# Routed mixture kernel: the first 256 columns of each upward block without a branch, two arms past them in place of seven widths

## The chip, the cores and the metric

The kernel runs on one core of one Trainium2 chip, and the metric is the time of one execution in device microseconds. Engines are named as the profile names them: PE (TensorE matmul), PEld (its weight loads), DVE (VectorE), ACT (ScalarE), POOL (GpSimd), SP (SyncE, which here only issues transfers).

## The reference

Three layers follow one another; all arithmetic is in f32. The change touches only the last one, a mixture of eight experts that sends each of 2304 tokens to one expert, with room for 576 tokens in each.

```python
kv  = einsum('bhsd,bhse->bhde', k, v)            # linear attention, then an RMS norm
x   = rmsnorm(einsum('bhsd,bhde->bhse', q, kv)) * g_norm
x   = relu(x @ w_in)**2 @ w_out                  # 2304 tokens, 512 -> 2048 -> 512
expert_idx = argmax(x @ w_gate, axis=1)          # 8 experts, capacity 576
# tokens are put into disp[e, slot] in their order, those past the capacity are dropped
h   = maximum(einsum('ecd,edf->ecf', disp, w1), 0)   # w1: 8 x 512 x 1024
y   = einsum('ecf,efd->ecd', h, w2)                  # w2: 8 x 1024 x 512
out[i] = gate_w[i] * y[expert_idx[i], slot[i]]
```

How many tokens an expert holds is known only while the kernel runs. With the inputs that are timed, the experts hold, in the order in which the kernel works on them (positions 0 to 7), 576, 167, 219, 576, 160, 391, 76 and 52 tokens.

## The kernel before, in words

A float32 product is done in three passes of float32r matmuls (high by high, high by low, low by high), so a block of 512 input features is 4 x 3 = 12 matmuls into one stretch of PSUM. Attention and the first mixture fill the first 486 us. After that comes the second mixture, one expert after another.

For each expert the kernel does an "up" stage and a "down" stage. The up stage has eight blocks f = 0 to 7 of 128 hidden features, two in each call of `up2` (i = 0 to 3). `up` multiplies the block of `w1` by the transposed tokens `x2` into `hb`, a PSUM tile of two banks of 512 columns (three such tiles take turns), and `put_g` writes the result to `g2`: ACT makes the relu's high part of 576 columns, DVE the low part. `put_last` has ACT copy the last half tile to `gl`. After each call, `next_pair` (not after the last) has ACT cast a freshly loaded 128x512 pair of weights and POOL subtract the cast from it; SP loads into four staging buffers ahead of that. The down stage multiplies `g2` by `w2`, tile of tokens by tile, each scaled on ACT and scattered by POOL.

An expert of at most 128 tokens takes the other arm of `up2`: `turned` computes the block with the tokens as the stationary operand, and the result is turned back by a transpose. Position 0 is special: most of its first 256 columns are done early, and `up_rest` does what is past them (320 columns here).

The work past the first mixture is in a section where every engine follows the order of the code (`tc.manual_schedule`). So the order of each engine's queue is the order of the calls in the loop over experts at its end, and SP's is that of `load_x` and `next_pair`. A `tc.If` compares a register with a number on each engine that has work in the block, and jumps. Both arms of it stand in the engine's instruction stream one after the other. `nothing` is a matmul of eight columns that stands in an arm without work.

The choice of width in the kernel before: `LEVELS` (line 526) has seven widths, `widths` (lines 815 to 823) searches them by halving, and each end of the search is an arm with its own 12 matmuls (24 for 576 columns). Where an arm is wider than a bank, its first 256 columns lie at column 256 of `hb`, otherwise at column 0. A register (`off`, loaded from `off_i`) tells ACT and DVE where to read.

Of the kernel before, what the change touches and what calls it, by code (L numbers as in the profile page):

```python
# [10 lines left out]
I32 = mybir.dt.int32  # L11
I64 = mybir.dt.int64
AF = mybir.ActivationFunctionType
ALU = mybir.AluOpType
# [5 lines left out]
P = 128  # L20
# [6 lines left out]
def attn_moe_kernel(ctx: ExitStack, tc: tile.TileContext, cap, kp, vp, qt, gn, wm, wg, wgt, w1, w2, ident, tri, out):  # L27
    nc = tc.nc
    B, NPAIR, _, NCH, _ = kp.shape
# [5 lines left out]
    E, NF2 = w1.shape[0], w1.shape[1] * 2  # L35
# [6 lines left out]
    NARROW, BANK, HALF = 256, 512, P // 2  # L42
# [4 lines left out]
    const = ctx.enter_context(tc.tile_pool(name="const", bufs=1))  # L47
# [8 lines left out]
    tri_sb = const.tile([P, 2, P], BF16, name="tri_sb")  # L56
    cnt = const.tile([P, E], F32, name="cnt")
    cnt_i = const.tile([P, E], I32, name="cnt_i")
    off_i = const.tile([P, E], I32, name="off_i")
    last_i = const.tile([P, E], I32, name="last_i")  # L60

    ek_i = const.tile([P, E], I32, name="ek_i")
# [460 lines left out]

    LAG, LEAD = 2, 4
    HOT = 9
    LEVELS = (NARROW, 304, 352, 400, 448, BANK, cap)
    units = []

    with tc.manual_schedule(engines={mybir.EngineType.SP}):
# [146 lines left out]
        for s in range(len(units)):  # L676
            j, f = units[s]
# [37 lines left out]
        v = nc.vector  # L715
# [3 lines left out]
        v.tensor_scalar(cnt, cnt, 1.0, -1.0, op0=ALU.max, op1=ALU.add)  # L719
        v.tensor_copy(last_i, cnt)  # L720
        v.tensor_scalar(last_i, last_i, 7, 7, op0=ALU.logical_shift_right, op1=ALU.logical_shift_left)
        v.tensor_scalar(off_i, cnt, float(BANK - 1), float(BANK - NARROW), op0=ALU.is_gt, op1=ALU.mult)
    ph1.close()


# [8 lines left out]
    hb = [psum[0].tile([P, 2 * BANK], F32, name=f"hb{i}") for i in range(3)]  # L734
# [23 lines left out]
    with tc.manual_schedule():  # L758
# [9 lines left out]
        ET = mybir.EngineType  # L768
# [7 lines left out]
        def nothing(ps, w):  # L776

            nc.tensor.matmul(ps[:w, :E], lhsT=tri_sb[:, 0, :w], rhs=tri_sb[:, 1, :E], start=True, stop=True)
# [20 lines left out]
        def w1_at(e, i, a, c):  # L799

            return we1[e, 2 * i + c // 2][:, a, c % 2 * 2 * P:(c % 2 + 1) * 2 * P]

        def part(e, f, h, o, w, x=x2):


            order = [(c, a, m) for c in range(KD) for a, m in PASSES]
            if f == 0:
                order = [(c, a, m) for a, m in ((0, 0), (1, 0), (0, 1)) for c in range(KD)]
            for k, (c, a, m) in enumerate(order):
                nc.tensor.matmul(  # L810
                    h, lhsT=w1_at(e, f // 2, a, c)[:, f % 2 * P:(f % 2 + 1) * P], rhs=x[:, m, c, o:o + w],
                    start=k == 0, stop=k == 3 * KD - 1,
                )

        def widths(e, levels, arm):

            mid = len(levels) // 2
            if not mid:
                return arm(levels[0])
            with tc.If(n[e] > levels[mid - 1]) as c:  # L820
                widths(e, levels[mid:], arm)
            with c.Else():
                widths(e, levels[:mid], arm)

        def up(e, f):

            h = hb[(e * NF2 + f) % 3]

            def arm(w):
                if w > BANK:  # L830
                    part(e, f, h[:, BANK - NARROW:BANK], 0, NARROW)
                    part(e, f, h[:, BANK:BANK + w - NARROW], NARROW, w - NARROW)
                else:
                    part(e, f, h[:, :w], 0, w)

            widths(e, LEVELS, arm)
            put_g(f, h[:, bass.ds(off[e], cap)], slice(0, cap))

        turned_sb = [ht_p.tile([P, 2 * P], F32, name=f"turned{i}") for i in range(2)]

# [10 lines left out]
        def up2(e, i):  # L851

            with tc.If(nall[e] > P) as many:  # L853
                up(e, 2 * i)
                up(e, 2 * i + 1)
            with many.Else():
                if i == 0:
                    nc.scalar.copy(turned_sb[0], turned(e, 0))
                if i + 1 < NF2 // 2:
                    s = turned(e, i + 1)  # L860
                hs = [hb[(e * NF2 + 2 * i + k) % 3][:, :P] for k in range(2)]
                for k, h in enumerate(hs):
                    nc.tensor.transpose(h, turned_sb[i % 2][:, k * P:(k + 1) * P], id_sb)
                if i + 1 < NF2 // 2:
                    nc.scalar.copy(turned_sb[(i + 1) % 2], s)
                for k, h in enumerate(hs):
                    put_g(2 * i + k, h, slice(0, P))
            for f in range(2 * i, 2 * i + 2):
                put_last(f, bass.ds(last[e], HALF))

        def put_g(f, src, cols):

            g = g2[f][:, :, cols]
            nc.scalar.activation(out=g[:, 0], in_=src, func=AF.Relu)  # L874
            nc.vector.scalar_tensor_tensor(  # L875
                out=g[:, 1], in0=src, scalar=0.0, in1=f32(g[:, 0]), op0=ALU.max, op1=ALU.subtract
            )
# [74 lines left out]
        for f in range(3):  # L952
# [5 lines left out]
            skip_runtime_bounds_check_because="an expert has no more than all tokens",  # L958
        )
        _, n = nc.values_load_multi_w_load_instructions(  # L960
            cnt_i[0:1, :], engines=[PE], min_val=0, max_val=cap,
            skip_runtime_bounds_check_because="the counts are clamped to the capacity on the chip",
        )
        _, nall = nc.values_load_multi_w_load_instructions(
            cnt_i[0:1, :], engines=[PE, ET.Activation, ET.DVE, ET.Pool], min_val=0, max_val=cap,
            skip_runtime_bounds_check_because="the counts are clamped to the capacity on the chip",
        )

        _, off = nc.values_load_multi_w_load_instructions(
            off_i[0:1, :], engines=[ET.Activation, ET.DVE], min_val=0, max_val=BANK - NARROW,  # L970
            skip_runtime_bounds_check_because="the offsets are one of two numbers",
        )

        _, last = nc.values_load_multi_w_load_instructions(
            last_i[0:1, :], engines=[ET.Activation], min_val=0, max_val=(cap - 1) // P * P,
            skip_runtime_bounds_check_because="the counts are clamped to the capacity on the chip",
# [11 lines left out]
        for e in range(E):  # L988
# [3 lines left out]
            if e == 0:  # L992
                with tc.If(early > NARROW - 1) as done:
                    for f in range(NF2):
                        up_rest(f)
                with done.Else():
                    tr_x(0, 0)
                    tr_x(0, 1)
                    for f in range(NF2):
                        up(0, f)  # L1000
                        put_last(f, bass.ds(last[0], HALF))
            else:
                for i in range(NF2 // 2):
                    up2(e, i)
                    if i < NF2 // 2 - 1:
                        next_pair((AP, AP))
# [69 lines left out]
```

## Time and profile before

| what | us |
|---|---|
| median of 3 runs (810.14 to 811.97) | 810.14 |
| the profiled execution's own time | 804.85 |
| its span, from the first to the last instruction | 803.1 |
| PE busy in the span | 729.3 |
| DVE, ACT, POOL busy | 371.1, 310.5, 291.5 |

The profiled execution is 5.3 us shorter than the median of the runs. All durations below come from it; a difference worked out in it is put on the median. The second mixture takes the last 317 us of the span. There each expert's up stage and down stage can be told apart by the matmuls: those of line 810 (up), 846 and 863 (the turned arm), and 907 (down).

### The profile page before, as it was taken

How to read it: one execution, taken by the hardware profiler on the slowest of the kernel's cores; microseconds unless marked ns; L12 is line 12 of the kernel's file. 1: busy time of each engine (PE TensorE's matmuls, PEld its weight loads, DVE VectorE, ACT ScalarE, POOL GpSimd, SP SyncE). 2: the span in 40 equal slices, each digit the busy share in tenths (PEclk: the TensorE clock that was granted, in tenths of full speed). 3: DMA queues.
4: the chain of work that ended last, by engine and by line, in shares of the span. 5: the costliest groups of instructions: out<-in, count | busy, mean ns of one | idle time of the engine just before them, and what ended most of it. 6: DMA issues, size and time to landing. Idle time of an engine off the chain costs nothing. (4 is left out here: it accounts for less than half of the span.)

```text
span 803.1 us, 12019 instructions
## 1 busy us (share of the span) xinstructions
PE 729.3 (91%) x3988; PEld 648.0 (81%) x3988; DVE 371.1 (46%) x829; ACT 310.5 (39%) x650; POOL 291.5 (36%) x288
## 2 busy tenths in 40 slices
PE   6788999999999999999999899997879997879663
PEld 6777999989999998899989788876768976777553
DVE  2999767279924943494469434202212202221101
ACT  2555454242223322322334533424635444544422
POOL 2575233030212002102104923253847373667440
PEclk9899999999999999999999999999969999999779
DMA  9937898020212012001004723353444454455400
GB/s 332 373 123 275 290 302 292 27 76 1 105 69 77 1 66 83 27 1 53 13 1 158 233 97 106 100 165 109 143 164 148 165 154 136 129 182 164 152 20 11
DMA packets 38044, 102.82 MB, mean 128 GB/s; under 512 B 4451, under 2 KB 4707, under 8 KB 37920
## 3 DMA queue, kind: packets, MB, share of 16 engines
q1 hardware_dynamic: 34912, 91.99, 35.0%
q0 software_dynamic: 3008, 9.10, 3.0%
q8 instruction: 87, 1.43, 0.8%
q14 instruction: 37, 0.30, 0.1%
HBM read 77.78 MB, written 23.91 MB: 127 GB/s over the span
## 5 line engine op out<-in xcount | busy, mean ns | idle before, releaser
L273 PE MATMUL pk<-xT,w 128*128 128x384 f32 x1152 | 223.1, 341 | 7.5 <-POOL w L183 4.6
L292 PE MATMUL pk<-w,g 128*128 128x512 f32 x864 | 218.3, 394 | 2.5 <-ACT g L284 2.5
L273 PEld LDWEIGHTS pk<-xT,w 128*128 128x128 f32 x1152 | 201.6, 188 | 17.3 <-POOL w L183 5.9
L194 POOL TENSOR_TENSOR w<-st,w 128x512 fp32r<-128x512 f32 x128 | 161.2, 1294 | 120.2 <-ACT w L190 120.2
L292 PEld LDWEIGHTS pk<-w,g 128*128 128x128 f32 x864 | 160.2, 188 | 31.7 <-ACT g L284 3.1
L810 PE MATMUL hb<-x,w 128*128 128x256 f32 (+2 forms) x672 | 105.5, 316 | 24.5 <-issue 11.3
L810 PEld LDWEIGHTS hb<-x,w 128*128 128x128 f32 x672 | 99.4, 203 | 29.9 <-issue 14.4
L875 DVE SCALAR_TENSOR_TENSOR g<-hb,g 128x576 fp32r<-128x576 f32 (+3 forms) x72 | 41.4, 586 | 147.6 <-ACT g L874 147.6
L281 ACT ACTIVATE rr<-pk 128x384 f32<-128x384 f32 x96 | 47.1, 491 | 154.2 <-PE pk L273 154.0
L283 DVE TENSOR_TENSOR pk<-pk,rr 128x384 f32<-128x384 f32 x96 | 54.0, 563 | 75.0 <-ACT rr L281 74.2
L102 POOL DMA_INDIRECT disp<-y,sli x18 | 19.0, 1058 | 173.5 <-DVE sli L409 52.9
L354 DVE SCALAR_TENSOR_TENSOR junk<-y,wgb 128x512 f32<-128x512 f32 x120 | 77.9, 684 | 0.6 <-ACT y L312 0.6
L190 ACT CAST w<-st 128x512 fp32r<-128x512 f32 x128 | 71.5, 620 | 11.6 <-DMA st<-in_w 11.2
L284 ACT CAST g<-pk 128x384 fp32r<-128x384 f32 x96 | 46.0, 479 | 72.2 <-DVE pk L283 71.8
L285 DVE TENSOR_TENSOR g<-pk,g 128x384 fp32r<-128x384 f32 x96 | 53.3, 556 | 36.3 <-ACT g L284 36.1
L183 POOL TENSOR_TENSOR w<-cf,w 128x512 fp32r<-128x512 f32 x32 | 46.8, 1481 | 61.4 <-ACT w L182 56.8
L907 PE MATMUL hb<-w,g 128*128 128x512 f32 x264 | 65.8, 407 | 3.2 <-DVEq L946 2.9
L907 PEld LDWEIGHTS hb<-w,g 128*128 128x128 f32 x264 | 50.2, 194 | 15.3 <-DVEq L946 3.2
L874 ACT ACTIVATE g<-hb 128x576 fp32r (+3 forms) x72 | 36.1, 515 | 66.3 <-PE hb L810 63.4
L102 POOL DMA_INDIRECT out<-o,meta x22 | 21.3, 968 | 56.5 <-DVEq L1019 22.6
L923 DVE SCALAR_TENSOR_TENSOR o<-bk,meta,o 64x512 f32<-64x512 f32 x3 | 2.3, 751 | 70.5 <-ACT o L922 50.6
L239 POOL TENSOR_SCALAR ms<-ss 128x8 f32<-128x8 f32 x18 | 4.6, 253 | 76.2 <-DVE ss L237 75.9
(134 smaller groups left out, 651.6 us busy)
## 6 DMA issues: line engine op xcount, KB each, us to landing
st<-in_w SPq DMA_DIRECT2D x64, 512.0 KB, 3.9
st<-in_wm SPq DMA_DIRECT2D x32, 512.0 KB, 6.9
disp<-zrow SPq DMA_DIRECT2D x9, 1028.0 KB, 11.2
xr<-disp SPq DMA_DIRECT2D x32, 257.0 KB, 4.8
k<-in_kp SPq DMA_DIRECT2D x16, 320.0 KB, 4.4
v<-in_vp SPq DMA_DIRECT2D x16, 320.0 KB, 4.1
q<-in_qt SPq DMA_DIRECT2D x18, 256.0 KB, 3.2
out<-zrow SPq DMA_DIRECT2D x9, 512.0 KB, 8.3
```

Source lines behind the costliest of these rows:

```text
L183: nc.gpsimd.tensor_tensor(w[:, 1, :], o, f32(w[:, 0, :]), op=ALU.subtract)
L190: nc.scalar.copy(w[:, 0, :], s[:, i, :])
L194: e.tensor_tensor(w[:, 1, :], s[:, i, :], f32(w[:, 0, :]), op=ALU.subtract)
L273: nc.tensor.matmul(h, lhsT=wi[f][:, a, c * P:(c + 1) * P], rhs=xT[j][:, m, c, :], start=n == 0, stop=n == 3 * KD - 1,)
L281: nc.scalar.activation(out=r, in_=h, func=AF.Relu)
L283: nc.vector.tensor_tensor(h, h, r, op=ALU.mult)
L284: nc.scalar.copy(g[:, 0, :], h)
L285: nc.vector.tensor_tensor(g[:, 1, :], h, f32(g[:, 0, :]), op=ALU.subtract)
L292: nc.tensor.matmul(ysets[j == 1][i], lhsT=g[:, a, i * P:(i + 1) * P], rhs=wo[f][:, m, :], start=f == 0 and n == 0, stop=f == NF - 1 and n ...
L354: nc.vector.scalar_tensor_tensor(out=junk, in0=yt[j * TB + i][:, :DM], scalar=1.0, in1=wgb[e // 2][:, e % 2, :], op0=ALU.mult, op1=ALU.mul ...
L810: nc.tensor.matmul(h, lhsT=w1_at(e, f // 2, a, c)[:, f % 2 * P:(f % 2 + 1) * P], rhs=x[:, m, c, o:o + w], start=k == 0, stop=k == 3 * KD - 1,)
L907: nc.tensor.matmul(ps[:k, :], lhsT=lhs(f, a), rhs=we2[e, f][:, b, :], start=n == 0, stop=n == len(passes) * NF2 - 1,)
```

## The change

Every up block of more than 128 tokens first does columns 0 to 255 without a branch. Then it asks whether the expert holds more than 256 tokens. If so, one of two arms does the next 160 (up to 416 tokens) or 320 columns; if not, a matmul of eight columns stands there. The first 256 columns always lie at column 256 of `hb`, so the register `off` and its loads go, and `put_g` reads at a fixed place. Widths in use for these inputs: 256 at positions 1, 2 and 4 as before; 256 and 320 at position 3 as before; at position 5 (391 tokens) 256 and 160 in place of 400.

```diff
-    off_i = const.tile([P, E], I32, name="off_i")
...
-    LEVELS = (NARROW, 304, 352, 400, 448, BANK, cap)
+    MIDDLE = 416
...
-        v.tensor_scalar(off_i, cnt, float(BANK - 1), float(BANK - NARROW), op0=ALU.is_gt, op1=ALU.mult)
...
-        def widths(e, levels, arm):
-
-            mid = len(levels) // 2
-            if not mid:
-                return arm(levels[0])
-            with tc.If(n[e] > levels[mid - 1]) as c:
-                widths(e, levels[mid:], arm)
-            with c.Else():
-                widths(e, levels[:mid], arm)
-
         def up(e, f):
 
-            h = hb[(e * NF2 + f) % 3]
-
-            def arm(w):
-                if w > BANK:
-                    part(e, f, h[:, BANK - NARROW:BANK], 0, NARROW)
-                    part(e, f, h[:, BANK:BANK + w - NARROW], NARROW, w - NARROW)
-                else:
-                    part(e, f, h[:, :w], 0, w)
-
-            widths(e, LEVELS, arm)
-            put_g(f, h[:, bass.ds(off[e], cap)], slice(0, cap))
+            h = hb[(e * NF2 + f) % 3][:, BANK - NARROW:]
+            part(e, f, h[:, :NARROW], 0, NARROW)
+            with tc.If(n[e] > NARROW) as more:
+                with tc.If(n[e] <= MIDDLE) as some:
+                    part(e, f, h[:, NARROW:MIDDLE], NARROW, MIDDLE - NARROW)
+                with some.Else():
+                    part(e, f, h[:, NARROW:cap], NARROW, cap - NARROW)
+            with more.Else():
+                nothing(h[:, NARROW:], P)
+            put_g(f, h[:, :cap], slice(0, cap))
...
-        _, off = nc.values_load_multi_w_load_instructions(
-            off_i[0:1, :], engines=[ET.Activation, ET.DVE], min_val=0, max_val=BANK - NARROW,
-            skip_runtime_bounds_check_because="the offsets are one of two numbers",
-        )
```

The first place is PE's queue in one up block. In the kernel before, the block begins with three comparisons, the arm of 256 and 320 columns, a jump and the arm of 512 columns; these are its last twelve rows (hb is the PSUM tile, x the transposed tokens, w the weights).

```order
L820 COMPARE_AND_BRANCH
L810 MATMUL hb_4468<-x_4489,w 128x448 x12
L820 UNCONDITIONAL_BRANCH
L810 MATMUL hb_4468<-x_4489,w 128x400 x12
L820 UNCONDITIONAL_BRANCH
L820 COMPARE_AND_BRANCH x2
L810 MATMUL hb_4468<-x_4489,w 128x352 x12
L820 UNCONDITIONAL_BRANCH
L810 MATMUL hb_4468<-x_4489,w 128x304 x12
L820 UNCONDITIONAL_BRANCH
L810 MATMUL hb_4468<-x_4489,w 128x256 x12
L820 UNCONDITIONAL_BRANCH
```

And this is the whole of the same block in the changed kernel.

```order
L808 MATMUL hb_4466<-x_4487,w 128x256 x12
L817 COMPARE_AND_BRANCH
L818 COMPARE_AND_BRANCH
L808 MATMUL hb_4466<-x_4487,w 128x160 x12
L818 UNCONDITIONAL_BRANCH
L808 MATMUL hb_4466<-x_4487,w 128x320 x12
L818 UNCONDITIONAL_BRANCH
L776 LDWEIGHTS tri_sb
L776 MATMUL hb_4466<-tri_sb 128x8
L817 UNCONDITIONAL_BRANCH
```

The block's matmuls in PE's stream fall from 96 to 37, and the 256-column matmuls move from its end, past six other arms, to its start.

The second place is ACT's queue in one call of `up2`, in the kernel before (rows from the comparison on 128 tokens to the end of the wide arm):

```order
L853 COMPARE_AND_BRANCH
L820 UNCONDITIONAL_BRANCH x2
L874 ISA
L874 ACTIVATE g_0_4473<-hb_4470 128x576
L874 REGISTER_ALU
L874 ACTIVATE g_1_4474<-hb_4468 128x576
L853 UNCONDITIONAL_BRANCH
```

And in the changed kernel:

```order
L840 COMPARE_AND_BRANCH
L817 UNCONDITIONAL_BRANCH
L861 ACTIVATE g_0_4471<-hb_4468 128x576
L817 UNCONDITIONAL_BRANCH
L861 ACTIVATE g_1_4472<-hb_4466 128x576
L840 UNCONDITIONAL_BRANCH
```

The two activations keep their place and size; the rows that put the register's value into their addresses are gone.

## Rows read from the trace of the kernel before

**Rows 1.** The page, busy time by engine: busy us (share) and instructions.
```profile
PE 729.3 (91%) x3988; PEld 648.0 (81%) x3988; DVE 371.1 (46%) x829; ACT 310.5 (39%) x650; POOL 291.5 (36%) x288
```

**Rows 2.** Waits of PE at line 810: total us, times, longest us.
```profile
PE hb L810 <- issue: 11.3, 11, 2.7
PE hb L810 <- DVE g L875: 10.5, 7, 2.2
```

**Rows 3.** Stretches, up stages of positions 1 to 7: length, busy by engine, clock, DMA.
```profile
544.70:564.40 19.70, 14.40 (x99) 13.06 (x98) 6.05 (x8) 9.61 (x20) 8.45 (x8) 0.91 0.23 66
...
574.70:601.40 26.70, 18.86 (x99) 17.50 (x99) 5.97 (x8) 11.88 (x24) 15.41 (x15) 0.68 0.53 172
...
615.00:640.60 25.60, 25.60 (x194) 25.60 (x194) 5.30 (x7) 11.90 (x24) 13.88 (x13) 1.00 0.47 157
...
667.80:688.60 20.80, 12.93 (x97) 11.83 (x97) 6.06 (x8) 9.73 (x20) 8.69 (x9) 1.00 0.25 73
...
699.80:722.90 23.10, 18.90 (x98) 17.13 (x97) 6.11 (x9) 12.53 (x26) 15.14 (x17) 1.00 0.60 181
...
745.40:761.00 15.60, 9.69 (x59) 8.77 (x60) 2.22 (x8) 7.60 (x25) 6.57 (x6) 0.80 0.44 144
...
775.00:791.00 16.00, 8.90 (x57) 8.09 (x57) 1.46 (x6) 4.21 (x18) 0.00 (x0) 0.89 0.03 9
```

**Rows 4.** Timeline of PE, position 1: start, us, instructions, idle before and its end.
```profile
544.78 3.99 PE L810 MATMUL hb<-x,w 128*128 128x256 f32 x32
...
553.16 1.69 PE L810 MATMUL hb<-x,w 128*128 128x256 f32 x12 [1.64 <-DVE g L875]
556.65 2.84 PE L810 MATMUL hb<-x,w 128*128 128x256 f32 x12 [1.80 <-DVE g L875]
...
562.83 1.70 PE L810 MATMUL hb<-x,w 128*128 128x256 f32 x12 [1.11 <-issue]
564.37 1.04 PE L789 MATMUL bk<-id_sb,xr 128*128 128x128 f32 x8
```

**Rows 5.** Timeline, position 2, around one stall of PE.
```profile
586.33 0.76 DVE L875 SCALAR_TENSOR_TENSOR g<-hb,g 128x576 fp32r<-128x576 f32 x1 [1.48 <-ACT g L874]
...
588.31 2.93 PE L810 MATMUL hb<-x,w 128*128 128x256 f32 x12 [2.70 <-issue]
```

**Rows 6.** Timelines of ACT (one pair of blocks) and POOL, position 1.
```profile
550.23 2.51 POOL L194 TENSOR_TENSOR w<-st,w 128x512 fp32r<-128x512 f32 x2 [2.52 <-ACT w L190]
...
550.58 0.64 ACT L874 ACTIVATE g<-hb 128x576 fp32r x1
551.56 0.65 ACT L874 ACTIVATE g<-hb 128x576 fp32r x1 [0.34 <-PE hb L810]
552.10 0.29 ACT L880 CAST gl<-g 128x128 fp32r x1
553.03 0.30 ACT L880 CAST gl<-g 128x128 fp32r x1 [0.64 <-DVE g L875]
553.24 1.14 ACT L190 CAST w<-st 128x512 fp32r<-128x512 f32 x2
```

**Rows 7.** Timeline of PE, unbroken runs: positions 0, 0, 3 and 5.
```profile
501.23 14.33 PE L810 MATMUL hb<-x,w 128*128 128x320 f32 x96
516.98 1.08 PE L789 MATMUL bk<-id_sb,xr 128*128 128x128 f32 x8 [1.42 <-issue]
...
614.98 25.82 PE L810 MATMUL hb<-x,w 128*128 128x256 f32 x192
...
699.89 4.58 PE L810 MATMUL hb<-x,w 128*128 128x400 f32 x24
```

**Rows 8.** Transfer queues in the first stretch of rows 3: packets, MB, share.
```profile
q8 instruction: 6, 0.10, 2.2%
```

**Rows 9.** Timeline of PE, position 7, the turned arm.
```profile
775.60 2.90 PE L846 MATMUL hb<-w,x 128*128 128x256 f32 x12 [3.49 <-issue]
...
782.61 1.66 PE L846 MATMUL bk<-w,x 128*128 128x256 f32 x12 [2.34 <-issue]
```

## The prediction

> **What bounds the kernel now.** I read the busy times first: PE is busy 91% of the span [rows 1], so only PE time can be saved, and the 9% in which it is idle is the first place to look. Then the waits of PE at line 810, the up blocks: the longest entry is "issue", in which PE waits for nothing that the profile shows, and DVE stands next [rows 2]. Then the stretches of the up stages [rows 3]: positions 1, 2 and 4, with 256 columns, take 19.7, 26.7 and 20.8 us, while position 3 does twice as many matmuls in 25.6 us without a gap. So the narrow stages aren't bound by matmuls. [...]
>
> The timeline tells what the gaps are. Position 1 has its first blocks back to back (32 matmuls), and then a block starts only every 3 to 3.5 us (553.16 to 556.65, on to 562.83) [rows 4]. One stall shows it best: DVE finishes at 587.09, the block before is long done, and PE starts the next at 588.31, marked "issue" [rows 5]. PE's own stream is late. The queue named "instruction" moves 6 packets of some 16 KB in the stage of position 1, one per 3.3 us [rows 8]: PE has to walk past 84 matmuls of arms that it doesn't take to reach its 12. In position 3 the same stream is hidden, since a block there has 3.2 us of matmuls to cover it (25.82 us for 8) [rows 7].
>
> DVE as the releaser I take as chance: with three tiles of hb a block needs the one three back, and in position 3 each block starts before ACT and DVE have begun on its predecessor, without a gap [rows 7].
>
> **The narrow positions 1, 2 and 4.** The change takes the skipped matmuls from 84 to 24 in a block, ahead of eight columns. Short jumps are free: at position 0 each block already jumps past a 12-matmul arm and one of eight columns, and 96 matmuls run in 14.33 us, 149 ns each, without a gap [rows 7]. With the turned arm (26 matmuls a pair of blocks, which these positions skip) the stage's stream falls from 8 x 96 + 4 x 26 = 872 matmuls to 8 x 37 + 104 = 400, so from 6 packets to about 2.8. At 3.3 us each that is 9 us (at 26.7 / 7 = 3.8 us, if position 2 fetched 7, some 11). I book what is late next, and then check it against this.
>
> Late next is ACT. For a pair of blocks it does two relus, two casts of gl, the second of which waits for DVE, and two weight casts: from 551.56 to 554.38, 2.8 us, and 0.6 us for the first relu, 3.4 us a pair [rows 6]. PE needs for two blocks 2 x 1.42 us (a 256-column matmul: twice 25.82 / 192 = 134 ns less the 149 ns of 320 columns, 120 ns, times 12) [rows 7], less than ACT.
>
> In position 1 ACT's work to 554.38 stays where it is. The third pair's relus then end by 555.6, DVE (0.76 us) and gl by 556.7, so PE starts the last block at about 556.4 and ends at 557.9, where it ended at 564.37 [rows 4, 6]: 6.5 us saved. Position 4 is the same case, 20.8 us to 13.1 plus the same lead of 0.1: 7.6 us. In position 2 the weight casts of the pairs before stand ahead of ACT's first relu; I add half of such a cast, 0.6 us [rows 6], so its stage becomes 13.1 + 0.6 = 13.7 us in place of 26.7: 13.0 us, about 6 of them the clock (18.86 us of busy PE against some 13) [rows 3]. Sum 27.1 us. The bounds: nothing, if the wait goes with the jump and not with its length; and 3 x 8 x 1.42 = 34 us left of 67.2, 33 us saved, if PE alone decides.
>
> The check: 9 to 11 us of packets stand under 13.1 to 13.7 us, so they fit, but not with much room. [...] I book 1 us for each of the three, 3 us in all (from 0 to 3 x 4).
>
> [...]
>
> **Position 5, 391 tokens.** 12 matmuls of 400 columns become 12 of 256 and 12 of 160. No row has 160 columns of float32r. From the rows at 256 (120 ns) and 320 (149) a line gives 120 - 96 x 0.45 = 77 ns; above, it can't cost more than the 320 columns do, 149. The nearest row in size, eight 128-column transposes, takes 1.08 us, 135 ns each with the last one's latency in it [rows 7]. I take 115. A block then costs 12 x (120 + 115) = 2.82 us, more than the 400-column one (24 in 4.58 us, 2.3 us a block [rows 7]), but it now covers the stream, and ACT's 1.7 us. 8 x 2.82 = 22.6 us and 0.2 of lead, where the stage took 23.1 us with its gaps [rows 3]: 0.3 us saved. Bounds: 77 ns gives 8 x 2.36 + 0.2 = 19.1, 4.0 saved; 149 ns gives 8 x 3.23 + 0.2 = 26.0, 2.9 lost.
>
> [...]
>
> **Positions 6 and 7, the turned arm.** Its own work is unchanged, but a call of up2 jumps past two up blocks to reach it: 192 matmuls before, 74 now, beside its own 26. The stages have 15.6 - 9.69 = 5.9 us and 16.0 - 8.90 = 7.1 us without PE [rows 3], and the long waits carry "issue" (3.49 and 2.34 us at position 7) [rows 9]. If the idle time goes with the length of the stream, (192 - 74) / (192 + 26) = 54% of 13.0 us go: 7.0 us. Bounds: 0, since casts and turned copies on ACT hold some of it; and 13.0, all.
>
> **Edits with no price.** Position 3 keeps its 24 matmuls a block, with two comparisons in the middle; it ran without a gap past three. The register loads, the rows that set addresses on ACT and DVE, and the small DVE operation for off_i go, on engines that wait for PE there (ACT 9.61 of 19.7 us busy, DVE 6.05 [rows 3]): nothing. The eight-column matmul ends the block later by some 0.05 us, 24 times, under ACT's pace; without that cover 1.2 us. SP's order is unchanged; the transfers of later weights and tokens come due earlier by what is saved.
>
> **Cover that may run out.** POOL needs 2.5 us for a pair of weights [rows 6], 20 us for an expert's 8 pairs, and with scatters and copies, which I estimate at 3 us, 23 us, where position 1 would take 13.1 + 10.3 = 23.4 us in all (10.3 from the end of its up stage to position 2). It fits, barely, and position 3 with 53 us lets it catch up.
>
> **The sum.** -27.1 + 3 - 0.3 - 7.0 = -31.4 us. The profiled execution took 804.85 us, so its like takes 773.4; it lies 5.3 us under the median of the runs, 810.14, and the median should become 778.7, say 779.
>
> **Rivals.**
> - The stream stays the bound. Each jump costs part of its wait whatever its length, because the next packet is asked for late; half of the narrow and turned savings remains, 17 us, and the time is 793. For it speaks that 9 to 11 us of packets stand under 13 us; against it position 0, where blocks of 1.8 us jump without a gap [rows 7]. [...]
> - Feeding becomes the bound. POOL's 23 us, and SP, which waits for POOL before it can load again, make ACT's weight casts late in positions 1, 2 and 5, and ACT's queue holds the relus behind them. Some 3 us each, 9 in all: 788. For it POOL's 15.41 of 26.7 us in position 2; against it the four staging buffers and the long position 3.
> - Slower. The second entry of rows 2 is right and PE waits in each narrow block for DVE and ACT; the stream was only in step with them. Then positions 1, 2 and 4 keep their length and gain 1.2 us of eight-column matmuls, position 5 loses 2.9, the turned arms keep theirs: 810.1 + 4.1 = 814. It decides if narrow blocks still start right after the DVE operation of the block before. Against it rows 5, where nothing runs for 1.2 us, and position 3.
> - The change does more: matmuls of 160 columns at 77 ns, the whole idle time of the turned arms, no residue: -31.4 - 3.7 - 6.0 - 3 = -44, 766.
>
> **How the numbers follow.** The forecast 0.60 (its own range 771 to 787), the stream 0.15, feeding 0.12, more 0.06, slower 0.04, and 0.03 for something between none and slower that I don't see. What can't be told from no change is 0.3%, 2.4 us. Faster: 0.60 + 0.15 + 0.12 + 0.06 = 0.93, of which I leave 0.03 to savings eaten up unseen: 0.90. Same 0.05, slower 0.05. The range runs from the forecast's lower side, with some of "more", to the stream's case: 768 to 797.
>
> **What would show it.** Right: the up stages of positions 1, 2 and 4 at 13 to 14 us, clock 1.00 in position 2, PE waits at the up line on ACT rather than issue, some 3 instruction packets a stage; position 5 at 22 to 23 us with 24 matmuls a block back to back; the turned stages at 11 to 13 us. Wrong: narrow blocks still 3 us apart, or 160 columns far from 115 ns. It would be wrong most of all if "issue" were something other than the fetch of skipped arms.

## The result, and the profile after

The changed kernel takes 762.48 us (median of 4 runs, 762.01 to 763.87), the kernel before, on the same chip, 811.06 us: 48.6 us less, a ratio of 0.9393 (95% interval 0.9355 to 0.9432). Faster was forecast, but 779 us, and 762.48 lies below the range of 768 to 797.

The page of the changed kernel, busy times and the queue that brings instructions:

```profile
PE 721.0 (95%) x4108; PEld 644.3 (85%) x4108; DVE 369.5 (49%) x828; ACT 309.8 (41%) x650; POOL 291.4 (38%) x288
...
q8 instruction: 58, 0.95, 0.5%
```

PE's share rises from 91% [rows 1] to 95%. It is busy 8 us less although 120 more matmuls run (4108 against 3988), since more of them run at the full clock (mean granted clock 0.986, before 0.968). The instruction packets fall from the 87 of the page of before to 58; in the stage of position 1 they fall from 6 [rows 8] to 3, as forecast. No wait at the up line (now 808) of 0.2 us or more is left among PE's waits, where 21.8 us stood in two entries [rows 2]. This is the longest that is left in the second mixture (total us, times, longest us). It stands ahead of the first matmul of position 7, where PE still waits on "issue":

```profile
PE hb L833 <- issue: 2.5, 1, 2.5
```

The up stages of the changed kernel, positions 1 to 7, each from its first matmul to the next stage's first (length, busy by engine, clock, DMA share, GB/s). The row 727.28:738.91 is the down stage of position 6, which stands between the two turned ones:

```profile
544.51:556.96 12.45, 12.45 (x105) 12.05 (x104) 5.11 (x7) 8.60 (x19) 6.08 (x6) 1.00 0.20 58
568.28:582.14 13.86, 13.05 (x106) 12.37 (x106) 5.02 (x7) 11.45 (x24) 13.28 (x12) 1.00 0.73 236
596.34:622.00 25.66, 25.66 (x194) 25.66 (x194) 5.30 (x7) 11.90 (x24) 13.88 (x13) 1.00 0.45 143
649.23:661.68 12.45, 12.45 (x106) 12.05 (x104) 5.11 (x7) 8.62 (x19) 6.07 (x6) 1.00 0.19 57
673.92:696.20 22.28, 22.28 (x194) 22.28 (x194) 6.05 (x8) 11.86 (x24) 14.95 (x17) 1.00 0.57 184
717.53:727.28 9.75, 7.68 (x58) 6.75 (x58) 2.22 (x7) 6.52 (x21) 5.07 (x5) 1.00 0.52 183
727.28:738.91 11.63, 8.12 (x33) 6.22 (x33) 1.78 (x4) 6.81 (x16) 11.24 (x12) 0.85 0.30 98
738.91:748.47 9.56, 8.54 (x57) 8.12 (x57) 1.47 (x6) 4.17 (x17) 0.79 (x1) 0.82 0.06 21
```

Against [rows 3]: the narrow stages have become 12.4, 13.9 and 12.4 us, PE busy through nearly all of them at a clock of 1.00, position 2 too, where it was 0.68. Position 3 is as before. The turned stages, 15.1 and 15.3 us in the trace of before when they are cut in the same way (in [rows 3], with some of the waiting ahead of them, 15.6 and 16.0), take 9.75 and 9.56 us.

One block of position 1 in the timeline of the changed kernel (start, us): the 12 matmuls, the eight columns, and at once the next block (at 552.26). Here the jump past 24 matmuls leaves no gap.

```profile
550.70 1.69 PE L808 MATMUL hb<-x,w 128*128 128x256 f32 x12
552.23 0.18 PE L776 MATMUL hb<-tri_sb 128*128 128x8 bf16 x1
```

ACT in the same stage, the first relus of three pairs of blocks, 3.37 and 3.38 us apart, the pace of 3.4 us that was worked out from [rows 6]:

```profile
550.48 1.18 ACT L861 ACTIVATE g<-hb 128x576 fp32r<-128x576 f32 x2
...
553.85 1.19 ACT L861 ACTIVATE g<-hb 128x576 fp32r<-128x576 f32 x2
...
557.23 1.18 ACT L861 ACTIVATE g<-hb 128x576 fp32r<-128x576 f32 x2
```

PE doesn't follow that pace: with three hb tiles it runs ahead at 1.56 us a block and is through at 556.96, and ACT's lag is paid at the start of the down stage, where PE waits 0.69 us for DVE.

The difference of the two spans, 42.5 us, splits as follows (starts of stages in both traces):

| part | us before | us after | change |
|---|---|---|---|
| up stages of positions 1, 2, 4 | 67.0 | 38.8 | -28.3 |
| what follows each of them | 35.2 | 37.8 | +2.6 |
| up stage of position 5 | 23.1 | 22.3 | -0.8 |
| turned stages (6 and 7) | 30.4 | 19.3 | -11.1 |
| between them | 15.1 | 11.6 | -3.5 |
| all else (1.1 of it between the up stages of positions 5 and 6) | | | -1.4 |

### The profile page after: what moved, and what is told of

It is laid out like the page before. It is cut to its first block, busy times and chain, and to the rows that moved or that the text cites. A ratio compares the mean times of both kernels' runs of the same rounds, so it can differ in the third digit from the quotient of the medians.

```text
span 760.6 us, 12136 instructions
## 1 busy us (share of the span) xinstructions
PE 721.0 (95%) x4108; PEld 644.3 (85%) x4108; DVE 369.5 (49%) x828; ACT 309.8 (41%) x650; POOL 291.4 (38%) x288
## 5 line engine op out<-in xcount | busy, mean ns | idle before, releaser
L272 PEld LDWEIGHTS pk<-xT,w 128*128 128x128 f32 x1152 | 201.6, 188 | 17.5 <-POOL w L182 6.3
L808 PE MATMUL hb<-x,w 128*128 128x256 f32 (+2 forms) x768 | 100.6, 290 | 0.1
L189 ACT CAST w<-st 128x512 fp32r<-128x512 f32 x128 | 71.5, 621 | 12.0 <-DMA st<-in_w 11.6
L861 ACT ACTIVATE g<-hb 128x576 fp32r<-128x576 f32 (+3 forms) x72 | 35.0, 513 | 36.4 <-PE hb L808 32.0
```

The source lines that it names most:

```text
L189: nc.scalar.copy(w[:, 0, :], s[:, i, :])
L272: nc.tensor.matmul(h, lhsT=wi[f][:, a, c * P:(c + 1) * P], rhs=xT[j][:, m, c, :], start=n == 0, stop=n == 3 * KD - 1,)
L808: nc.tensor.matmul(h, lhsT=w1_at(e, f // 2, a, c)[:, f % 2 * P:(f % 2 + 1) * P], rhs=x[:, m, c, o:o + w], start=k == 0, stop=k == 3 * KD - 1,)
```

## Experiments

Two theories were to be told apart: that the gain is the length of PE's instruction stream (matmuls of arms that aren't taken must still be walked past), and that it is one of the other edits (the part without a branch, fewer comparisons, the fixed place without a register). Inside the first, the size of the turned stages' part was open.

**Three widths in the kernel before.**

```diff
-    LEVELS = (NARROW, 304, 352, 400, 448, BANK, cap)
+    LEVELS = (NARROW, 400, cap)
...
-                if w > BANK:
+                if w > 400:
...
-        v.tensor_scalar(off_i, cnt, float(BANK - 1), float(BANK - NARROW), op0=ALU.is_gt, op1=ALU.mult)
+        v.tensor_scalar(off_i, cnt, float(400 - 1), float(BANK - NARROW), op0=ALU.is_gt, op1=ALU.mult)
```

> The kernel before with one thing shortened: three widths (256, 400, 576) in place of seven, so that PE's stream holds 48 matmuls a block, not 96. The comparisons ahead of the matmuls, the register that tells where to read, and the place at column 0 stay as they were. If the length of the skipped stream is the cause, the narrow stages run without gaps (12 to 13 us each) and position 5 does 12 matmuls of 400 columns a block in some 18 to 19 us where the changed kernel takes 22.3; the turned stages skip 96 matmuls a call and not 74, perhaps 1 to 2 us worse: about 761. If the part without a branch, or the fixed place without the register, is the cause, the narrow stages stay at 20 to 27 us: about 800 to 811.

Measured: 758.49 us against 808.56 for the kernel before, ratio 0.9393 (0.9349 to 0.9436). The narrow stages take 12.2, 13.4 and 12.2 us, with the comparisons ahead of the matmuls, the register and column 0 still there. So neither the part without a branch nor the fixed place makes the gain. This run can't rule out that it is the fewer comparisons, since it too makes one in place of two on the way to 256 columns. The runs with 24 and 60 skipped matmuls below rule it out: both make two, and only the second loses the gain. The stages of positions 1, 5 and 6 of this run:

```profile
542.42:554.61 12.19, 11.96 (x97) 11.60 (x96) 5.11 (x7) 8.52 (x19) 6.00 (x5) 1.00 0.20 59
...
671.18:688.72 17.54, 17.54 (x98) 17.50 (x98) 6.05 (x8) 11.60 (x24) 13.96 (x15) 1.00 0.72 231
709.90:722.00 12.10, 9.19 (x59) 8.25 (x58) 2.22 (x7) 6.55 (x21) 5.17 (x5) 0.86 0.53 177
```

Position 5 takes 17.5 us with whole 400-column matmuls, not 22.3; the first turned stage, which skips 96 matmuls a call, is 2.3 us longer than with 74, with a wait of 2.2 us on "issue" in its middle and a clock of 0.86.

**The stream made long again, first attempt.**

```diff
             with more.Else():
-                nothing(h[:, NARROW:], P)
+                with tc.If(n[e] > cap) as never:
+                    for _ in range(5):
+                        part(e, f, h[:, NARROW:cap], NARROW, cap - NARROW)
+                with never.Else():
+                    nothing(h[:, NARROW:], P)
```

> The changed kernel with 60 matmuls of 320 columns a block that are never run (they stand behind a comparison with more tokens than an expert can hold), at positions 1 to 7: 97 matmuls a block in PE's stream, as in the kernel before. All that is executed stays, but for one comparison and jump in narrow blocks. If the length of the stream is the cause, nearly all of the gain goes: narrow stages back to 20 to 27 us, turned stages to 15, 800 to 811 in all. If the gain came from the fixed place, from fewer comparisons or from the part without a branch, 762 to 765.

> The same 60 matmuls that are never run, but at positions 6 and 7 alone. It measures the term that was forecast at 7.0 us. By the forecast's sizing (idle time in proportion to the stream) 769.5; by the two traces, in which the stages of positions 6 and 7 and what lies between them are 14.6 us shorter, 777; if the turned stages gained from something else, 763.

Measured: 763.39 and 762.90 us. These say nothing against the stream. The instruction packets are 59 and 58, as in the changed kernel, so the 60 matmuls are not in PE's stream. The likely reason is that the comparison with 576 could be decided when the program was built, since the register is declared to hold at most 576. The two are in effect repeats of the changed kernel; the edit was made again with a number that can't be decided at build.

**The stream made long again, second attempt.**

```diff
-                with tc.If(n[e] > cap) as never:
+                with tc.If(n[e] > 300) as never:
```

> The changed kernel, and in the arm of the eight columns a further comparison (more than 300 tokens, which is never so there) ahead of 60 matmuls of 320 columns: 97 matmuls a block in PE's stream at positions 1 to 7, as in the kernel before. Unlike the run e2_pad_all they stand in the program this time (PE's program has them, and the instruction packets should rise from 58 to 85 or so). If the length of the skipped stream is the cause, the gain goes: the stages of positions 1, 2 and 4 back to 20 to 27 us, the turned ones to 15, about 800 to 811. If it isn't, 763 to 765 (a comparison and a jump more in narrow blocks).

Measured: 811.59 us, against 808.47 for the kernel before: ratio 1.0045 (1.0002 to 1.0087). All of the gain is gone, with no executed matmul added, and the packets are back at 85 (in the stage of position 1 there are 5, in the changed kernel 3). The timeline of position 1 shows it: the eight columns, which stand behind the skipped matmuls, now come 1.0 and 2.7 us late, and PE waits for "issue".

```profile
553.82 0.18 PE L776 MATMUL hb<-tri_sb 128*128 128x8 bf16 x1 [1.02 <-issue]
553.86 1.67 PE L808 MATMUL hb<-x,w 128*128 128x256 f32 x12
558.24 0.18 PE L776 MATMUL hb<-tri_sb 128*128 128x8 bf16 x1 [2.71 <-issue]
```

Its stages at positions 1, 2, 4 and 5, of which the first three read like [rows 3]:

```profile
544.76:565.30 20.54, 14.86 (x105) 13.42 (x103) 5.96 (x8) 9.62 (x20) 8.73 (x9) 0.87 0.25 73
578.13:601.60 23.47, 17.68 (x106) 16.06 (x106) 6.05 (x8) 11.88 (x24) 13.61 (x13) 0.78 0.51 169
668.26:690.25 21.99, 15.95 (x105) 14.79 (x104) 6.05 (x8) 9.81 (x20) 8.66 (x9) 0.84 0.21 61
701.56:727.50 25.94, 24.14 (x195) 23.97 (x194) 6.06 (x8) 12.04 (x25) 15.10 (x17) 0.93 0.51 162
```

Position 5, whose 2.8 us of matmuls a block were thought to cover a long stream, loses 3.7 us as well. So 23 ns a matmul (worked out below) is too little for it: 880 matmuls at that price are 20.2 us, less than the 22.3 us of its own work.

**At positions 6 and 7 alone.**

```diff
+                if e >= 6:      # the 60 matmuls; at other positions the eight columns alone
```

> The same 60 matmuls at positions 6 and 7 alone. If the turned stages' gain is the length of the stream, as large as the two traces show it, 14 to 15 us are lost, 777; if it is as the forecast sized it, 7 us, 769.5; if it had another cause, 762.5. The stretch from the first turned matmul of position 6 to the last of position 7 was 46 us before and is 31 us after.

Measured: 778.20 us (776.24 to 779.16), 14.4 to 15.7 us above the changed kernel (763.85 and 762.48 in two other sessions). So the turned arms' share is twice what was forecast. The stages of position 6, the stretch between, and position 7:

```profile
718.30:734.10 15.80, 9.56 (x57) 8.60 (x58) 2.22 (x7) 7.83 (x23) 6.50 (x6) 0.76 0.47 149
734.10:744.90 10.80, 7.56 (x34) 6.08 (x33) 1.79 (x4) 5.80 (x13) 10.03 (x11) 0.82 0.12 43
744.90:763.70 18.80, 11.66 (x56) 10.41 (x57) 1.46 (x6) 4.12 (x17) 0.61 (x1) 0.67 0.06 14
```

They sum to 45.4 us, as in the kernel before (46 us), and not to the 30.9 of the changed one. How the loss divides between them isn't the same in each trace: here the stretch between is short and position 7 long.

**How long a stream is too long.**

```diff
+                if e in (1, 2, 4):      # 24, then 36 matmuls that are never run
```

> 24 such matmuls at positions 1, 2 and 4 alone: 61 a block. By the packets of the kernel before (3.3 us each, 872 matmuls in 6) a matmul in the stream costs 23 ns, so a block of 61 and its share of 13 for the turned arm needs 1.7 us, just over the 1.56 us that its own matmuls take: the stages stay within 1 us of 12.4 and 13.9 us, 763 to 766 in all. If every skipped matmul costs, not only those past this mark, some 24/60 of the way back: 12.4 to 16 us a stage, 774.

> 36 matmuls of the arm that is never run at positions 1, 2 and 4: 73 a block, between 61 (no cost in the time, first stalls in position 2) and 97 (all of the gain lost). At 23 ns each, with the turned arm's share of 13, a block's stream takes 2.0 us against 1.56 of matmuls; the first three blocks or so run free, so some 5 x 0.4 = 2 us a stage are lost, and up to 3 us where transfers run beside it: 768 to 771. If a short stream is a matter of a mark and not of its length, either 763 or 790.

Measured: 762.82 us with 24 (61 matmuls a block), 771.54 us with 36 (73 a block; the changed kernel in the same session 763.85). The stages of the first at positions 1, 2 and 4:

```profile
544.37:557.59 13.22, 12.95 (x106) 12.10 (x104) 5.14 (x7) 9.57 (x20) 6.85 (x6) 1.00 0.23 65
568.12:584.01 15.89, 13.33 (x107) 12.38 (x106) 5.78 (x8) 11.87 (x25) 15.25 (x15) 1.00 0.74 253
650.65:665.14 14.49, 12.88 (x105) 12.19 (x104) 5.87 (x8) 9.79 (x21) 8.09 (x7) 1.00 0.27 87
```

They are 0.8, 2.0 and 2.0 us longer, so the mark is passed already in two of them by more than the 1 us expected. That the whole time doesn't show these 4.8 us is in part luck: 2.1 come back in what follows the three stages, and 1.8 between the starts of positions 6 and 7, where the wait of 2.5 us on "issue" of the changed kernel's trace is missing in this one. The second:

```profile
545.47:560.88 15.41, 13.18 (x106) 12.31 (x104) 5.70 (x8) 9.88 (x21) 7.48 (x7) 1.00 0.28 82
571.30:591.47 20.17, 13.56 (x107) 12.45 (x106) 5.96 (x8) 11.78 (x24) 14.14 (x13) 1.00 0.63 213
658.06:673.26 15.20, 13.22 (x105) 12.25 (x104) 5.96 (x8) 10.00 (x21) 8.64 (x9) 1.00 0.27 85
```

3.0 and 2.8 us more at positions 1 and 4, and 6.3 at position 2. 771.5 stands at the upper end of the 768 to 771 expected from 23 ns a matmul.

The three lengths have the same jumps, so it isn't a price per jump. A stage's stream holds eight blocks and the 104 matmuls of the turned arm: 592, 688 and 880 matmuls with 24, 36 and 60 skipped ones, which at 23 ns are 13.6, 15.8 and 20.2 us. The stages of positions 1 and 4 took 13.2 and 14.5, 15.4 and 15.2, 20.5 and 22.0 us. Over these and the two traces of the kernel before the price is 22 to 26 ns a matmul. At position 2 it is 27 to 31; the transfers are heavier there (253 and 213 GB/s in the two traces above), but whether they slow the stream wasn't tested.

**The price of 160 columns.**

```diff
-    MIDDLE = 416
+    MIDDLE = 392
```

> The changed kernel with 136 columns in the middle arm in place of 160 (up to 392 tokens; position 5 holds 391). If such a matmul is bound by its columns, at 0.45 ns each between 256 and 320, 96 matmuls lose 24 x 0.45 = 11 ns each, and the stage of position 5 falls from 22.3 to 21.2 us. If it is bound by the load of its weights, nothing changes: 22.3 us. The whole time is 762 either way, to within its scatter.

Measured: 761.42 us (two runs, 758.28 and 764.56), and in the trace position 5 takes what it took:

```profile
676.39:698.61 22.22, 22.22 (x195) 22.22 (x194) 6.05 (x8) 11.86 (x24) 14.98 (x17) 1.00 0.56 184
```

136 columns cost as much as 160. With the 120 ns for 256 columns that follow from [rows 7], the estimate is (22.28 / 8 - 12 x 0.120) / 12 = 112 ns each for 160, and 111 from the 22.22 us here. So columns don't set the price between these two sizes. Whether the load of the weights does isn't shown: the runs show the price and not its cause.

**The kernel before, once more.**

> The kernel before, once more, for a second trace of it. The profile that the forecast was worked out in took 804.85 us, the runs 810.14 at the median. If the 5.3 us lie in the stalls of the second mixture, its stages differ between the two traces by some us; if they lie ahead of it, the first block of position 1 starts at another time than 544.78 us and the stages agree within 1 us.

Measured: 807.09 us, a span of 805.3. Position 1 starts at 544.93 us (544.78 in the first trace), so almost nothing differs ahead of it. Its stages at positions 1, 2, 4 and 6 are these:

```profile
544.93:564.05 19.12, 13.03 (x98) 11.81 (x96) 6.05 (x8) 9.71 (x20) 8.70 (x9) 1.00 0.24 70
574.36:597.86 23.50, 14.61 (x98) 13.02 (x98) 5.96 (x8) 12.19 (x25) 15.19 (x14) 0.93 0.60 193
666.09:689.00 22.91, 16.23 (x97) 15.24 (x96) 6.05 (x8) 9.71 (x20) 8.69 (x9) 0.77 0.26 81
...
746.30:763.30 17.00, 10.72 (x58) 9.40 (x56) 2.21 (x7) 6.57 (x21) 5.91 (x5) 0.72 0.43 132
```

Position 2 is 3.2 us shorter than in [rows 3], position 4 is 2.1 longer, with the clock the other way round: 0.93 and 0.77 here, 0.68 and 1.00 there. The stalls, and the granted clock of the stages they fall in, differ from one execution to the next. Even position 3, which ran without a gap in [rows 7], has two waits on "issue" here, so its 3.2 us of matmuls a block don't always cover the long stream:

```profile
624.77 3.46 PE L810 MATMUL hb<-x,w 128*128 128x256 f32 x24 [0.20 <-issue]
628.81 10.21 PE L810 MATMUL hb<-x,w 128*128 128x256 f32 x72 [0.58 <-issue]
```

**A version put together from this.** The short stream, and 257 to 400 tokens whole at column 0, with the register kept.

```diff
+        v.tensor_scalar(lo, cnt, float(NARROW - 1), float(BANK - NARROW), op0=ALU.is_le, op1=ALU.mult)
+        v.tensor_scalar(hi, cnt, float(MIDDLE - 1), float(BANK - NARROW), op0=ALU.is_gt, op1=ALU.mult)
+        v.tensor_tensor(off_i, lo, hi, op=ALU.add)
...
+            with tc.If(off[e] < 1) as middle:
+                part(e, f, h[:, :MIDDLE], 0, MIDDLE)
+            with middle.Else():
+                low()     # 256 columns, then 320 or the eight columns
```

> A version put together from what the runs showed: the stream as short as in the changed kernel (37 matmuls a block), and 257 to 400 tokens in one piece of 400 columns at column 0, as in the kernel before, with the register that tells where to read. Position 5's stage should take 17.6 us, as in the run with three widths, and not 22.3 (4.7 less); the turned stages as in the changed kernel. 758 against 762.5. If the register or the place cost anything on ACT or DVE, the narrow stages are longer than 12.4 and 13.9 us.

> The changed kernel once more, beside the other two on the same chip: 762.5 us, stages of positions 1, 2, 4 and 5 at 12.4, 13.9, 12.4 and 22.3 us.

Measured: 757.18 us (756.41 to 758.18), ratio to the kernel before 0.9318 (0.9277 to 0.9359); the changed kernel in the same session 763.85 us (763.30 to 766.03). It beats both. Positions 1, 5 and 7:

```profile
547.81:560.25 12.44, 12.44 (x105) 12.04 (x104) 5.11 (x7) 8.61 (x19) 6.08 (x6) 1.00 0.20 59
...
677.25:694.78 17.53, 17.53 (x98) 17.49 (x98) 6.06 (x8) 11.60 (x24) 13.97 (x15) 1.00 0.73 230
...
734.80:742.97 8.17, 7.45 (x57) 6.68 (x57) 1.47 (x6) 3.99 (x17) 3.33 (x3) 1.00 0.08 27
```

Position 5 gives the 4.7 us. The narrow stage is as long with the register as without it. In the session's trace of the changed kernel the stages are as expected: 12.4, 13.9, 12.4 and 22.3 us. Of the other 2 us by which the new version is ahead no edit is the known cause: in its trace the stretch from the end of position 6's stage to the end of position 7's is 3.0 us shorter, and it starts position 1 1.2 us later; how much of this is scatter isn't known.

## Why the prediction was wrong, point by point

- **What bounds it: right.** That the arms not taken hold up PE's stream is shown by four runs: shortening them in the kernel before gives the gain (758.49 us), 60 matmuls a block that are never run take it back (811.59 us), and 24 and 36 of them take nothing and some 8 us of the whole time. The bound that the wait goes with the jump and not with its length didn't hold.
- **DVE as the releaser by chance: right.** The narrow blocks now start 1.56 us apart, and no such wait is left. ACT and DVE do the same work in the run with 60 skipped matmuls, and there the blocks are late again. The rival that ends slower is gone with it.
- **Narrow positions: the size near, in part by luck.** 27.1 less 3 for a residue was forecast. The stages gave 28.3, and 2.6 came back behind them: 25.7. That the stream was the cost is right. But ACT was to be late next and to hold PE in the stage, and it doesn't: with three hb tiles PE waits at no up block, and its own 1.56 us a block set the stage's length. The 3 us for a residue of stalls were an estimate that no run shows: in the changed kernel PE is busy for all of the 12.45 us at positions 1 and 4, and for 13.05 of 13.86 at position 2. In place of such a residue ACT's lag is paid at the start of the down stage (0.7 us at positions 1 and 4), and at position 2 a wait of 0.7 us for the transferred tokens.
- **Position 5: right.** 0.3 us was forecast, 0.8 measured; 115 ns for 160 columns was taken, and the measured stage gives 112; the 77 ns of the columns alone would have been far off.
- **Positions 6 and 7: the step that failed.** "If the idle time goes with the length of the stream", 54% of 13.0 us, 7.0 us. The traces show 11.1 in the stages and 3.5 between them, 14.6 in all, and the run with the 60 matmuls at these positions alone 14.4 to 15.7, above even the bound of 13.0. Three things were wrong. First, the stalls didn't shrink in proportion to the stream: the idle time went from 13.0 to 3.1 us, by three quarters and not by 54%. Second, the stretch between the two stages was put at nothing, though most of the wait of 3.49 us of [rows 9], which the prediction names, stands there, outside the stretches of [rows 3]. Third, PE's busy time was taken as fixed, though in [rows 3] the clock stood at 0.80 and 0.89. The two stages and the stretch between, before:

```profile
744.81:760.48 15.67, 9.17 (x58) 8.25 (x58) 2.22 (x7) 7.52 (x23) 6.05 (x6) 0.82 0.44 146
760.48:775.60 15.12, 8.69 (x33) 6.73 (x33) 1.78 (x4) 5.92 (x14) 11.08 (x11) 0.73 0.17 54
775.60:790.93 15.33, 8.83 (x57) 7.99 (x57) 1.46 (x6) 4.13 (x17) 0.00 (x0) 0.90 0.03 6
```

Position 6's busy time fell from 9.17 to 7.68 us as its clock came to 1.00; position 7 gained only 0.3 us, at a clock of 0.82. For position 2 the clock (0.68 in [rows 3]) had been counted.
- **From the profile to the median: wrong too.** "It lies 5.3 us under the median of the runs", and the difference was carried over. But the two traces of the kernel before differ in the stages that stall, and hardly ahead of them; and where no stall is left the stages agree, 12.4, 13.9, 12.4 and 22.3 us in both traces of the changed kernel. A run with more stalls than the profiled one would thus gain more by the change, and both would come down to about the same time; no run shows that the 5.3 us were stalls. The changed kernel's profiled execution took 762.38 us, its median is 762.48. Of the 16.5 us by which the forecast of 779 was too slow, 11.1 are the sum (42.5 in place of 31.4): 7.6 at positions 6 and 7, 1.6 at the narrow ones, 0.5 at position 5 and 1.4 elsewhere. Another 5.2 are this step, and the rest is rounding.
- **The rivals.** "The stream stays the bound" didn't happen at 37 matmuls a block, and it is what happens at 73. Of "feeding" little shows: the 2.6 us behind the narrow stages are for the most part ACT's own pace, and only the wait for the tokens at position 2, 0.7 us, is a late transfer.

## What to carry to other kernels

Here a matmul of an arm that isn't taken cost PE's stream 22 to 26 ns at positions 1 and 4, and the 12 matmuls that a block runs (1.56 us) covered a stream of 37 matmuls a block (12.45 us a stage) but not one of 73 (15.41 and 15.20 us). So where a run-time choice stands in a loop that is written out, compare the matmuls skipped with those run, and look for waits on "issue" while all else is idle. A few arms were enough: three widths do what seven did (758.49 us against 808.56), and a finer width that saves columns pays only if its arm doesn't lengthen the stream past the cover. With the stalls went the lower clock (0.68 to 1.00 at position 2, 0.82 to 1.00 at position 6, though not at position 7), so size such a gain by the stage's own work at a clock of 1.00, not by a share of its idle time. And take it off the time of the execution in which it was worked out: the difference between that execution and the median, 5.3 us here, can be stalls, which would go too.

## What the runs showed of the hardware

- A skipped matmul costs PE's stream 22 to 26 ns at positions 1 and 4: 97 a block against 12 to run (1.56 us) loses all of the gain, 73 some 8 us, 61 nothing in the time of two runs, though the three stages are 4.8 us longer. With the 3776 matmuls taken out of the program (59 in each of 64 blocks, with those of an arm of position 0 that isn't taken) 29 packets of 16 KB (0.95 MB in the 58 that are left) went (87 to 58), 126 bytes for each.
- Jumps themselves are nearly hidden: with 24 matmuls skipped in each block, the next block's first matmul follows 0.03 to 0.04 us after the start of the eight columns at positions 1 and 4, and 0.03 to 0.29 us after it at position 2.
- A float32r matmul of 136 columns takes 111 ns and one of 160 takes 112, by an estimate from the stages of position 5 (22.22 and 22.28 us, less 120 ns for each matmul of 256 columns, from [rows 7]).
- The kernel before took 802.67 to 811.88 us in 13 runs beside each other, the changed one 762.01 to 763.87 in its 4. That the scatter goes with the stalls isn't shown by this: two versions with a short stream scatter by 5 to 6 us as well, the one with 136 columns (758.28 and 764.56) and the one with three widths (756.24 to 761.39).
